# Attention beside an MLP on one core: products with v in groups of four, and all eight PSUM banks given out by a model

## The chip, the cores and the metric

The kernel runs on one core of a Trainium2 chip. The metric is the device time of one execution in microseconds (us), as the median of several executions. The core has engines with a queue of their own each: TensorE (matrix products, PE in the profile; its weight loads are PEld), VectorE (DVE), ScalarE (ACT), GpSimd (POOL), and SyncE (SP), which here only issues DMAs. TensorE writes its products to PSUM, which has eight banks of 128 partitions by 512 float32 numbers. A bank can be written again only when VectorE or ScalarE has read the last product out of it.

## The reference

For 2048 tokens of width 576 the reference computes an attention layer of 32 heads (18 numbers per head) and an MLP of inner width 4608 on the same input, and mixes the two with a gate per token:

```python
def _A_ref(x, wqkv, wo):
    B, S, D = x.shape
    H = 32; Dh = D // H
    qkv = (lambda x, *d: x.transpose(*d))((x @ wqkv).reshape(B, S, 3, H, Dh), 2, 0, 3, 1, 4)
    q, k, v = qkv[0], qkv[1], qkv[2]
    scale = Dh ** -0.5
    scores = jnp.einsum("bhqd,bhkd->bhqk", q, k) * scale
    p = _softmax(scores, axis=-1)
    o = jnp.einsum("bhqk,bhkd->bhqd", p, v)
    return (lambda x, *d: x.transpose(*d))(o, 0, 2, 1, 3).reshape(B, S, D) @ wo

def _B_ref(x, w1, b1, w2, b2):
    y = _layernorm(x, axis=-1)
    h = _gelu(jnp.einsum("bsd,df->bsf", y, w1) + b1)
    return jnp.einsum("bsf,fd->bsd", h, w2) + b2

x = A_x
g = _sigmoid((x * gate_w).sum(-1, keepdims=True))
a = _A_ref(x, A_wqkv, A_wo)
b = _B_ref(x, B_w1, B_b1, B_w2, B_b2)
return g * a + (1 - g) * b
```

## The kernel before

**Stages.** A first stage (to about 245 us) projects q, k and v, prepares the normalized input of the MLP and begins the first MLP products. The main loop carries attention and the MLP together. The rest projects the attention output and mixes (`out_proj`, products on L1353).

**Attention.** The work is cut into 32 units (`NU`): a pair of heads by half of the queries (1024). A unit needs the maximum of every row of scores before its exponentials. So scores are computed twice. A *round* (`s1_round`, products on L234) computes scores for 128 queries by 512 keys for both heads and takes their maxima on VectorE (L236); a unit has 32 rounds. When the last round of a unit has been taken, `s1_finish` turns the maxima into two more rows of the query tile `qa`: `parts` on ScalarE, `rows` on VectorE (L257, L258), and eight small DMAs from the tile `mr` (issued by `dma_r`, L141). They are deferred by counts of *slots*; every call of `run_due` is one slot. With these rows in `qa` the second scores (`s2`, L320) come out with the maximum taken off, and ScalarE's exponential reads them from PSUM and writes the ring buffer (L322). The 512 steps of the main loop are 32 units by 16 blocks of 128 keys; a step has two calls of `s2`, one for each 512 queries. Each call can take a round along (`loop_round`). Rounds run a few calls ahead of the unit that needs them (`LEAD`, 4). When none are left, the kernel calls itself `bare`.

**Products with v** (`pv`, L350) take the exponentials of finished steps and sum them up in one bank per unit. They use the array in another shape: four products of 32 output rows each, side by side, where all score and MLP products use half of the rows each. The ring holds four steps (three from `NARROW` on). In the loop a run of `pv` stands after the first `s2` of a step, in place of an MLP piece. It comes when three steps are finished (`room`, 2 near the end), or when the MLP piece before it ended an MLP unit (`ended`) and at least one step is finished.

**MLP.** It is a generator, `mlp()`. Its units are `h_pair` (two blocks of 128 inner columns, 27 pairs of products on L611, then GELU by ScalarE, VectorE and GpSimd) and `out_pair` (128 tokens by 576, 24 pairs of products on L751, then two additions on VectorE, L721). 36 groups hold two `h_pair` and four `out_pair` each. `fill` draws the next piece after a call of `s2`; where a unit is cut into pieces is set by `ends`. `cut[0]` is 1 at the end of a piece, 2 at the end of a unit, 3 where the next product's input isn't there yet. `spent` and `behind` compare the MLP's progress with its due time.

**Banks.** Six banks are given out by a model (`Earliest`): each has the time at which its reader will be done (`let_go`), by clocks of TensorE, VectorE and ScalarE that the program keeps while it writes the instructions (`pe_t`, `dve_t`, `act_t`). They serve scores, rounds and the sums of `pv`. Two more (`ps_w`) belong to the MLP while rounds are left. The order of instructions on each engine is the one written; semaphores make them wait.

Of the kernel before, what the change touches and what calls it, by code (L numbers as in the profile page):

```python
# [58 lines left out]
NARROW = 431  # L59
# [4 lines left out]
def gated_mix_kernel(ctx: ExitStack, tc: tile.TileContext, x, wqkv, wo, w1, b1, w2, b2, gate_w, out):  # L64
# [97 lines left out]
    def run_due(ns=SLOT):  # L162

        slot[0] += 1
        now[0] += ns
# [74 lines left out]

    def s1_finish(u):
# [7 lines left out]
        def parts():  # L249
# [3 lines left out]
            defer(2 if looped[0] else 8, rows)  # L253

        def rows():
# [11 lines left out]
            for n in range(8):  # L267
                if aside:
                    defer(1 + n, lambda n=n: store(*divmod(n, 4)))
                else:  # L270
                    store(*divmod(n, 4))
        defer(3 if looped[0] else 2, parts)
# [36 lines left out]
    def s2(u, kc, qb, around, ns):  # L309

        flush()
        qa, ka = QA[u % 3], k_tile(UNITS[u][0])
# [26 lines left out]
    def pv(n0, n1):  # L339

        flush()
        for c in range(n0, n1):
# [9 lines left out]
            pe_t[0] += 1040.0  # L352
# [38 lines left out]
    def take_round():  # L391
        u, r = rounds.pop()
        head = s1_round(u, r)
        if r == NR - 1:
            defer(1, lambda: s1_finish(u))
# [10 lines left out]
    lent = [0]  # L406
    extra = [LEAD]
# [12 lines left out]
    def mlp():  # L420
# [129 lines left out]

        def cuts(n, pieces):
# [3 lines left out]
        turns = [0]  # L555

        def pair_of_banks(own):

            if own:
                return [psum(ps_w) for _ in range(2)], ()  # L560
# [6 lines left out]
        def banks(q):  # L567

            if q % 2 and not looped[0]:
                return pair_of_banks(False)  # L570
            return wide_banks()

        def wide_banks():

            if rounds:
                return pair_of_banks(True)
            turns[0] += 1
            return pair_of_banks(turns[0] % 2 == 0)

        def give_back(ids):  # L580
            for b in ids:
                let_go(b, dve_t, 480.0)

        def h_pair(q, last, inner=False):
# [8 lines left out]
            ps, ids = banks(q)  # L593
# [6 lines left out]
            late = spent[0] < behind[0]  # L600
            if room[0] == 3:
                ends = cuts(27, max(1, 5 - piece[0]))
            else:
                ends = cuts(27, (5, 5, 4)[piece[0]] if last else (3, 5, 4)[piece[0]])
                if (last or spent[0] > behind[0] + AHEAD) and piece[0] == 0 and not late:

                    ends = {4, 9, 14, 18, 23}
# [29 lines left out]
            engine(act_t, 690.0)  # L637
            give_back(ids)
# [841 lines left out]
```

## Time and profile before

| | us |
|---|---|
| median of 3 runs | 2214.97 (2214.9 to 2216.17) |
| profiled execution | 2215.03 |
| its span, first to last instruction | 2213.1 |
| ScalarE busy | 1436.3 (65%) |
| VectorE busy | 1644.7 (74%) |
| GpSimd busy | 949.1 (43%) |
| first product with v | at 260.0 |
| last product with v | at 2161.4 |

How to read the profile: the page has the busy time of every engine, groups of instructions by line of the kernel, and what ended the idle time before them. The timeline lists instructions in order of time: start in us, length in us, engine, line, operation, output<-inputs, and how many alike were merged (x8). A number in brackets is idle time of the engine before the instruction, with what released it. Instructions of one shape on both halves of the array run at the same time, so that starts tell more than lengths do. The windows view has, for a stretch, its length and then the busy time (and count) of PE, PEld, DVE, ACT and POOL, the granted TensorE clock (1.00 is full), the DMA share and GB/s.

### The profile page before, as it was taken

Reading aid. Unit: us, or ns where it says so; the run is one execution under the profiler, and the core shown is the slowest. Engines: PE = TensorE matmul, PEld = TensorE weight load, DVE = VectorE, ACT = ScalarE, POOL = GpSimd, SP = SyncE. Lnnn points to the kernel's source line nnn. Section 1 sums busy time; section 2 is a strip of 40 time slices with the busy share of each in tenths; the row PEclk is TensorE's granted clock in tenths of the full one; section 3 lists DMA queues with packets and bytes.
Section 4 is the critical chain, followed back from the end, with each engine's and each line's share of the span. In section 5 each row is a group of like instructions: output and inputs, shape, how many; then the busy total and the mean of one; then the engine's idle time right before and its main releaser. Section 6 shows DMA issues by size and latency. Waiting matters only on the chain. (4 is left out here: it accounts for less than half of the span.)

```text
span 2213.1 us, 51656 instructions
## 1 busy us (share of the span) xinstructions
PE 2196.4 (99%) x20569; PEld 1599.6 (72%) x20569; DVE 1644.7 (74%) x2887; ACT 1436.3 (65%) x2719; POOL 949.1 (43%) x936
## 2 busy tenths in 40 slices
PE   8999999999999999999999999999999999999999
PEld 7878777777767777677677676776677677777668
DVE  5675777777777777777777777777777777787844
ACT  4223677777776666666666666666766667666771
POOL 4002566666663444444445444444534444444420
PEclk9999999999999999999999999999999999999999
DMA  7755654536485423342273424243563333333355
GB/s 241 259 190 188 206 172 140 171 133 179 152 230 184 127 102 122 101 145 92 104 187 141 125 100 124 101 126 120 137 187 113 135 113 106 116 109 117 97 177 182
DMA packets 163414, 323.65 MB, mean 146 GB/s; under 512 B 59838, under 2 KB 86370, under 8 KB 152338
## 3 DMA queue, kind: packets, MB, share of 16 engines
q1 hardware_dynamic: 159462, 313.60, 44.4%
q10 hardware_dynamic: 3712, 6.75, 0.8%
q8 instruction: 162, 2.65, 0.5%
q14 instruction: 78, 0.64, 0.1%
HBM read 229.07 MB, written 95.16 MB: 147 GB/s over the span
## 5 line engine op out<-in xcount | busy, mean ns | idle before, releaser
L236 DVE TENSOR_REDUCE m<-ps 128x1 f32<-128x512 f32 x2048 | 1307.5, 684 | 392.0 <-PE ps L234 354.9
L322 ACT ACTIVATE p<-ps 128x512 f32<-128x512 f32 x1080 | 582.6, 596 | 283.4 <-PE ps L234 188.8
L322 ACT ACTIVATE ring<-ps 128x512 f32<-128x512 f32 x968 | 523.2, 596 | 259.5 <-PE ps L234 186.5
L320 PE MATMUL ps<-qa,ka 56*128 56x512 f32 x2048 | 685.9, 409 | 4.5 <-DMA qa<-mr 2.6
L234 PE MATMUL ps<-ka,qa 54*128 54x512 f32 x2048 | 625.6, 409 | 0.9 <-DVE big L968 0.7
L611 PE MATMUL ps<-big,w 64*128 64x512 f32 x3888 | 516.5, 392 | 0.1
L320 PEld LDWEIGHTS ps<-qa,ka 56*128 56x128 f32 x2048 | 358.4, 185 | 212.0 <-DVE m L236 130.8
L751 PE MATMUL ps<-w,hh 64*128 64x288 f32 x4352 | 491.2, 293 | 0.9 <-ACT z L636 0.8
L187 POOL TENSOR_SCALAR zz<-zz 128x512 f32<-128x512 f32 x272 | 169.2, 622 | 742.7 <-ACT zz L702 714.1
L751 PEld LDWEIGHTS ps<-w,hh 64*128 64x128 f32 x4352 | 418.1, 186 | 22.1 <-ACT z L636 1.2
L611 PEld LDWEIGHTS ps<-big,w 64*128 64x128 f32 x3888 | 380.6, 185 | 72.2 <-ACT vt L1066 0.3
L187 POOL TENSOR_TENSOR zz<-zz,z 128x512 f32<-128x512 f32 x280 | 361.8, 1293 | 35.9 <-ACT zz L705 9.8
L751 PE MATMUL ps<-w,hl 64*128 64x288 f32 x2176 | 340.7, 293 | 0.0
L234 PEld LDWEIGHTS ps<-ka,qa 54*128 54x128 f32 x2048 | 318.2, 186 | 23.1 <-issue 3.6
L350 PE MATMUL ps<-p,vt 128*32 128x512 f32 x2160 | 265.2, 598 | 0.0
L350 PE MATMUL ps<-ring,vt 128*32 128x512 f32 x1936 | 238.9, 598 | 0.0
L751 PEld LDWEIGHTS ps<-w,hl 64*128 64x128 f32 x2176 | 236.9, 186 | 0.0
L187 POOL TENSOR_TENSOR w<-x,w 128x576 fp32r<-128x576 f32 (+1 forms) x34 | 68.2, 2009 | 271.2 <-ACT w L490 206.6
L187 POOL TENSOR_TENSOR hl<-zz,hh 128x512 fp32r<-128x512 f32 x134 | 174.6, 1304 | 14.0 <-ACT hh L664 3.2
L350 PEld LDWEIGHTS ps<-p,vt 128*32 128x32 f32 x2160 | 57.9, 109 | 126.8 <-issue 124.2
L350 PEld LDWEIGHTS ps<-ring,vt 128*32 128x32 f32 x1936 | 52.3, 109 | 112.2 <-issue 111.2
L1037 PE MATMUL ps<-big,wqk 128*128 128x512 f32 x504 | 123.5, 400 | 0.0
(120 smaller groups left out, 1452.0 us busy)
## 6 DMA issues: line engine op xcount, KB each, us to landing
w<-w_scr SPq DMA_DIRECT2D x54, 1152.0 KB
w<-w_scr SPq DMA_DIRECT2D x108, 576.0 KB
w_scr<-w SPq DMA_DIRECT2D x18, 1152.0 KB
w_scr<-w SPq DMA_DIRECT2D x36, 576.0 KB
qa<-qk_scr SPq DMA_DIRECT2D x192, 72.0 KB
ka<-qk_scr SPq DMA_DIRECT2D x90, 144.0 KB
big<-y_scr SPq DMA_DIRECT2D x48, 256.0 KB
x<-in_B_w_dram SPq DMA_DIRECT2D x34, 288.0 KB
```

Source lines behind the costliest of these rows:

```text
L187: fn(*args, **kw)
L234: nc.tensor.matmul(ps, qa[r0:r0 + 54, t * P:(t + 1) * P], ka[r0:r0 + 54, kb * TB:(kb + 1) * TB], start=True, stop=True)
L236: nc.vector.tensor_reduce(M4[u][:, h, t, kb:kb + 1], ps, axis=AX.X, op=ALU.max)
L320: nc.tensor.matmul(ps, ka[r0:r0 + 56, kc * P:(kc + 1) * P], qa[r0:r0 + 56, qb * TB:(qb + 1) * TB], start=True, stop=True)
L322: nc.scalar.activation(ring(n)[:, qb, h], ps, AF.Exp, scale=SCALE)
L350: nc.tensor.matmul(OB[u][0][r:r + 32, :], v[:, k, 19 * h:19 * h + 32], ring(c)[:, qb, h, :], start=(k == 0), stop=(k == NT - 1))
L611: nc.tensor.matmul(ps[h], wt[w_][r, c, :], Y[s_][r, c, :], start=(k == 0), stop=(k == 26))
L751: mm = nc.tensor.matmul(ps[nn][:, :ND], h_[r, tok], w_[p_][r, cs[nn]], start=(k == 0 or bare and k == 3 * G), stop=(k == 6 * G - 1 or bare ...
L1037: nc.tensor.matmul(ps, w_[:, c, ms], big[:, s_, :], start=(k == 0), stop=(k == len(prods) - 1))
```

## The change

The loop no longer puts the run of `pv` where an MLP unit ends. It counts steps alone: `GROUP` 4 below step 432, then 3. The run stands at the end of a step and includes that step. All eight banks are in the model, and the MLP takes its two from it as well. Rounds are no longer tied one to a call: `loop_round` leaves one out when the model sees no four banks free, and `spare_round` puts one in between, so that the lead floats between 6 and 10. `now`, the program's time for deferred work, is TensorE's model clock in the loop. Pieces of the MLP are cut by its progress (`pace`). The parts of `s1_finish` are registered in `FINISH`, and `s2` runs what is left of them before a unit starts.

```diff
-NARROW = 431
+NARROW = 432
+GROUP = 4
+AHEAD_MIN = 6
+AHEAD_MAX = 10
+ENTER = 310.0
+PV_NS = 925.0
@@ run_due @@
-        now[0] += ns
+        now[0] = pe_t[0] if looped[0] else now[0] + ns
@@ s1_finish @@
+    def in_turn(u, n, fn):
+        def once():
+            if once in FINISH[u]:
+                FINISH[u].remove(once)
+                fn()
+        FINISH[u].append(once)
+        defer(n, once)
+
+    def finished(u):
+        while FINISH[u]:
+            FINISH[u][0]()
...
-            defer(2 if looped[0] else 8, rows)
+            in_turn(u, 2 if looped[0] else 4, rows)
...
-        defer(3 if looped[0] else 2, parts)
+        in_turn(u, 3 if looped[0] else 2, parts)
@@ s2 @@
         flush()
+        finished(u)
@@ pv @@
         flush()
+        pe_t[0] += ENTER
...
-            pe_t[0] += 1040.0
+            pe_t[0] += PV_NS
@@ rounds @@
-    def lend_round():
-        if rounds and not lent[0]:
-            next_round()
-            lent[0] = 1
-
-    def loop_round():
-        if lent[0]:
-            lent[0] = 0
-        elif rounds:
-            return take_round()
+    lead = [LEAD]
+    must = [0]
+
+    def fits(n, tol):
+        return sorted(free_at)[n - 1] <= pe_t[0] + tol
+
+    def loop_round():
+        if not rounds:
+            return None
+        if must[0] or lead[0] <= AHEAD_MIN or lead[0] <= AHEAD_MAX and fits(4, 300.0):
+            must[0] = 0
+            return take_round()
+        lead[0] -= 1
+        return None
+
+    def spare_round(n, tol):
+        if rounds and lead[0] < AHEAD_MAX and fits(n, tol):
+            lead[0] += 1
+            next_round()
+            return True
@@ mlp @@
+        def pace():
+            d = spent[0] - behind[0]
+            return 0 if d < 0 else 1 if d < AHEAD else 2
...
-            if own:
-                return [psum(ps_w) for _ in range(2)], ()
+        def wide_banks():
             tiles, ids = [], []
             for _ in range(2):
                 tiles.append(psum(ps_x))
                 ids.append(taken[0])
             return tiles, ids
@@ h_pair @@
-            if room[0] == 3:
-                ends = cuts(27, max(1, 5 - piece[0]))
-            else:
-                ends = cuts(27, (5, 5, 4)[piece[0]] if last else (3, 5, 4)[piece[0]])
...
+            ends = cuts(27, 4 + pace() + (open_pairs[0] if looped[0] else 0))
...
-            engine(act_t, 690.0)
-            give_back(ids)
+            let_go(ids[0], act_t, 690.0)
+            let_go(ids[1], dve_t, 750.0)
@@ out_pair @@
+            ends = {7, 15} if bare else {6, 12} if pace() == 0 else {6, 12, 18}
...
+                        if k == 12 and not bare:
+                            must[0] = 1
+                        elif k == 18 and 18 not in ends and not bare:
+                            spare_round(4, 100.0)
@@ banks @@
-    for i in range(4, 6):
+    for i in range(4, 8):
         bank_x.append(ctx.enter_context(tc.tile_pool(name=f"ps_x{i}", bufs=1, space=PSUM)))
         free_at.append(pe_t[0])
-    ps_w = ctx.enter_context(tc.tile_pool(name="ps_w", bufs=2, space=PSUM))
@@ fill @@
-            ended[0] = atom() == 2
-            piece[0] += 1
-            run_due(max(spent[0] - t, GAP))
+            if atom() == 3:
+                spare_round(4, 100.0)
+            run_due()
@@ main loop @@
+    shift = now[0] - pe_t[0]
+    for clock in (pe_t, act_t, dve_t):
+        clock[0] += shift
+    free_at[:] = [t + shift for t in free_at]
...
-            room[0] = 3 if step < NARROW - 3 else 2
...
             s2(u, kc, 0, loop_round(), 462.0)
-            if step - done[0] >= room[0] or room[0] == 3 and ended[0] and step > done[0]:
-                pv(done[0], step)
-                done[0] = step
-                piece[0] = 0
-                ended[0] = 0
-            else:
-                fill(step)
-            s2(u, kc, 1, loop_round(), 462.0)
-            if not (room[0] == 3 and ended[0]):
+            fill(step)
+            s2(u, kc, 1, loop_round(), 462.0)
+            if step + 1 - done[0] >= (GROUP if step < NARROW else GROUP - 1):
+                spare_round(2, 200.0)
+                pv(done[0], step + 1)
+                done[0] = step + 1
+            else:
                 fill(step)
```

More of the change, by code (lines that the diff above doesn't have):

```diff
@@ L239, in s1_round @@
         return head
+    FINISH = {u: [] for u in range(NU)}
+    def in_turn(u, n, fn):
[8 more added lines that the diff above has]
+            FINISH[u][0]()
     def s1_finish(u):
@@ L565, in pair_of_banks @@
             return tiles, ids
[L567 to L578, printed above, removed]
         def give_back(ids):
             for b in ids:
-                let_go(b, dve_t, 480.0)
+                let_go(b, dve_t, 450.0)
         def h_pair(q, last, inner=False):
@@ L592, in h_pair @@
             del W1[q]
-            ps, ids = banks(q)
+            ps, ids = wide_banks()
             if q == 0:
@@ L599, in h_pair @@
             loaded = 0
-            late = spent[0] < behind[0]
-            if room[0] == 3:
-                ends = cuts(27, max(1, 5 - piece[0]))
-            else:
-                ends = cuts(27, (5, 5, 4)[piece[0]] if last else (3, 5, 4)[piece[0]])
-                if (last or spent[0] > behind[0] + AHEAD) and piece[0] == 0 and not late:
-                    ends = {4, 9, 14, 18, 23}
+            ends = cuts(27, 4 + pace() + (open_pairs[0] if looped[0] else 0))
             for k, (w_, s_, c) in enumerate(slots):
@@ L723, in out_pair @@
             ps, ids = wide_banks()
-            ends = {7, 15} if piece[0] == 0 else cuts(24, max(1, 3 - piece[0]))
-            folded = piece[0] == 0 and not bare
-            if folded:
-                ends = {6, 12}
+            ends = {7, 15} if bare else {6, 12} if pace() == 0 else {6, 12, 18}
             k = 0
@@ L736, in out_pair @@
                 elif turn == 1:
-                    if 3 * G not in ends:
-                        lend_round()
                     turned[0] += 2
@@ L762, in out_pair @@
                         k += 1
-                        if folded and k == 6:
-                            if extra[0]:
-                                extra[0] -= 1
-                            else:
-                                lent[0] = 1
-                        if folded and k == 18:
-                            next_round()
+                        if k == 12 and not bare:
+                            must[0] = 1
+                        elif k == 18 and 18 not in ends and not bare:
+                            spare_round(4, 100.0)
                         if k < 6 * G:
@@ L856, in gated_mix_kernel @@
     cut = [0]
-    piece = [0]
-    room = [2]
     behind = [0.0]
@@ L1328, in out_proj @@
         opened[0] = True
-        banks = 0
         for b in range(NB):
@@ L1342, in out_proj @@
                         if 0 in cut_:
-                            ps[t, n] = psum((ps_x, ps_w)[banks % 2])
-                            own[t, n] = None if banks % 2 else taken[0]
-                            banks += 1
+                            ps[t, n] = psum(ps_x)
+                            own[t, n] = taken[0]
                         for c in cut_:
@@ L1363, in out_proj @@
                                                        op0=ALU.mult, op1=ALU.add)
-                        if own[t, n] is not None:
-                            let_go(own[t, n], dve_t, 480.0)
+                        let_go(own[t, n], dve_t, 480.0)
                         yield 122.5
@@ L1390, in gated_mix_kernel @@
     next(proj)
-    ended = [0]
     def fill(step):
```

8 lines of the change are left out of this document (2 added, 6 removed).

## The prediction

> **What bounds the kernel now.** I read the page's engine shares first, then the waits of TensorE, then the stretches, and last the timeline of TensorE around single instructions. The page, its first engine row:
>
> ```profile
> PE 2196.4 (99%) x20569; PEld 1599.6 (72%) x20569; DVE 1644.7 (74%) x2887; ACT 1436.3 (65%) x2719; POOL 949.1 (43%) x936
> ```
>
> The waits of TensorE (engine, line, what it waited for: total us, times, longest), cut to four rows:
>
> ```profile
> PE ps L320 <- DMA qa<-mr: 2.6, 2, 1.8
> PE ps L320 <- DVE x L721: 1.7, 1, 1.7
> ...
> PE ps L751 <- ACT z L636: 0.8, 1, 0.8
> ...
> PE ps L320 <- ACT p L322: 0.2, 1, 0.2
> ```
>
> The stretches (length, then busy us of PE, PEld, DVE, ACT, POOL, granted clock):
>
> ```profile
> 400.00:1200.00 800.00, 800.00 (x7950) 569.03 (x7944) 618.10 (x1066) 563.63 (x1073) 406.44 (x404) 1.00 0.45 145
> ```
>
> TensorE is the bound: 99% of the span, all 800 of 800 us in the middle of the loop at clock 1.00. There VectorE is busy 77% (618.10 of 800) and ScalarE 70%. So in the loop an edit is worth what it takes out of, or puts into, TensorE's own row. That row can still be shortened without removing one product, because a busy TensorE isn't evenly fast. The timeline of TensorE around a run of products with v (L350; eight records, x8, are one step), first with three steps and then with two:
>
> ```profile
> 305.87 1.06 PE L350 MATMUL ps<-ring,vt 128*32 128x512 f32 x8
> 306.75 1.90 PE L350 MATMUL ps<-p,vt 128*32 128x512 f32 x16
> 308.58 0.50 PE L320 MATMUL ps<-qa,ka 56*128 56x512 f32 x1
> ...
> 327.83 0.40 PE L320 MATMUL ps<-qa,ka 56*128 56x512 f32 x1
> 327.84 0.40 PE L234 MATMUL ps<-ka,qa 54*128 54x512 f32 x1
> 328.16 1.92 PE L350 MATMUL ps<-ring,vt 128*32 128x512 f32 x16
> 330.02 0.50 PE L320 MATMUL ps<-qa,ka 56*128 56x512 f32 x1
> 330.02 0.73 PE L234 MATMUL ps<-ka,qa 54*128 54x512 f32 x2
> 330.36 0.39 PE L320 MATMUL ps<-qa,ka 56*128 56x512 f32 x1
> 330.59 0.43 PE L751 MATMUL ps<-w,hh 64*128 64x288 f32 x4
> ```
>
> Score products come as pairs, one on each half of the rows, and and a pair normally takes 0.23 us until the next products start (330.36 to 330.59). The run of three lasts 308.58 - 305.87 = 2.71 us, the run of two 330.02 - 328.16 = 1.86 us; so **one step of products with v costs 0.85 us, and every run 0.16 us besides** (1.86 - 2 x 0.85). The pair ahead of a run takes 0.33 us (327.83 to 328.16), the first behind it 0.34 us (330.02 to 330.36), some 0.10 us too much each. **A run therefore costs 0.36 us for being a run.** The whole trace has 226 runs on TensorE, 166 of two steps and 60 of three (166 x 2 + 60 x 3 = 512); the first, and the last, in its two pieces:
>
> ```profile
> 260.02 1.92 PE L350 MATMUL ps<-p,vt 128*32 128x512 f32 x16
> ...
> 2159.42 1.06 PE L350 MATMUL ps<-p,vt 128*32 128x512 f32 x8
> 2160.30 1.65 PE L350 MATMUL ps<-ring,vt 128*32 128x512 f32 x8
> ```
>
> **The change, part by part.** *Runs of four.* The new loop counts steps alone: one run per four steps below step 432 (108 runs), then per three up to 510 (26), and one of two behind the loop: 135 runs, 91 fewer. Products, weights and their number stay. 91 x 0.36 = **32.8 us off TensorE's row**. Nothing else was under those 0.36 us, since TensorE is the bound; they go off the span unless TensorE then waits.
>
> *Start of the loop.* The row maxima of unit 0 are finished four slots earlier (4 in place of 8 for `rows`). What that moves, in the timelines of TensorE, VectorE and SP's queue:
>
> ```profile
> 246.68 0.43 PE L751 MATMUL ps<-w,hl 64*128 64x288 f32 x2
> 247.89 0.47 PE L320 MATMUL ps<-qa,ka 56*128 56x512 f32 x1 [0.78 <-DMA qa<-mr]
> 247.89 0.71 PE L234 MATMUL ps<-ka,qa 54*128 54x512 f32 x2
> 250.42 0.79 PE L320 MATMUL ps<-qa,ka 56*128 56x512 f32 x1 [1.82 <-DMA qa<-mr]
> ```
> ```profile
> 242.18 1.29 DVE L236 TENSOR_REDUCE m<-ps 128x1 f32<-128x512 f32 x2 [0.35 <-PE ps L234]
> 243.39 0.18 DVE L257 TENSOR_REDUCE nm<-nm 128x16 f32<-128x32 f32 x1
> 243.67 0.21 DVE L258 STREAM_TRANSPOSE mr<-nm 128x32 f32<-128x32 f32 x1
> ```
> ```profile
> 243.91 5.42 SPq L141 DMA_DIRECT2D qa<-mr  x8
> ```
>
> A turn of the loop ahead has three slots and one round, so four slots put L257, L258 and the eight DMAs ahead of the pair of maxima that starts at 242.18: about 1.3 us of maxima and their 0.35 us of waiting, some 1.8 us with the gap behind. SP's queue takes the eight (5.42 us) that much earlier and passes nothing on which the start waits. The second half's product at 250.42 comes 1.8 us earlier: **-1.8 us**. Behind these waits lies a slow stretch:
>
> ```profile
> 246.40:249.80 3.40, 1.42 (x12) 0.66 (x8) 2.58 (x4) 2.81 (x6) 2.97 (x3) 1.00 0.03 5
> 249.80:260.10 10.30, 9.65 (x59) 7.88 (x63) 5.88 (x11) 7.01 (x13) 4.14 (x4) 0.50 0.71 145
> 2094.40:2097.80 3.40, 1.82 (x22) 1.34 (x20) 2.53 (x7) 3.18 (x7) 0.00 (x0) 1.00 0.01 2
> ```
>
> After 3.4 us with 1.42 us busy the granted clock was 0.50 for 10.3 us, which costs half of it, 5.1 us. A like stretch with 1.82 us busy (third row) was followed by none. With 1.8 us less waiting the first has about 2.3 us busy by the same products, so the drop may go; I leave it in the sum and keep -5.1 us for the range.
>
> *Banks and rounds.* This adds waits that the old trace doesn't show. Before, six banks carried scores, maxima and the output of a unit, and two belonged to the MLP; the run with v stood where an MLP unit ended, so that the two were read out under it. Now a run stands anywhere and eight banks go round: one holds the unit's output, two the open MLP product, two may still wait for the additions (L721) of the last. Three are then left where scores and a round want four. Behind a product that waits stands everything on TensorE, in order. VectorE's and ScalarE's pace, from their timelines:
>
> ```profile
> 1003.59 2.52 DVE L236 TENSOR_REDUCE m<-ps 128x1 f32<-128x512 f32 x4 [0.86 <-PE ps L234]
> 1006.02 0.81 DVE L721 SCALAR_TENSOR_TENSOR x<-ps,x 128x288 f32<-128x288 f32 x2
> ```
> ```profile
> 1002.52 2.12 ACT L322 ACTIVATE ring<-ps 128x512 f32<-128x512 f32 x4 [0.18 <-PE ps L320]
> ```
>
> A maximum takes 0.63 us, a bank's two additions 0.81 us, an exponential 0.53 us. Four steps last about 14.5 us and hold 16 maxima (10.1 us) and some two pairs of additions (1.7 us): 11.8 us of VectorE; its run with v is 4 x 0.85 + 0.36 = 3.8 us, so of the other 10.7 us VectorE must have 1.1 us in hand as the run begins: two full banks. The added spare round ahead of each run is just that. ScalarE's 16 exponentials take 8.5 us. On the mean it fits, but with little room. The price of the new waits is bounded below by nothing (226 old periods show 0.2 us of waiting for an exponential in all; a gain is excluded, since there is no bank wait to remove but the 1.7 us of L721), and above by one maximum for each of the 144 MLP output units, 144 x 0.63 = 91 us. The round is left out or moved where the model sees no bank, with a tolerance of 0.3 us, so I take the value near the lower end: 0.3 us at half of the 36 MLP groups, where a first product must wait for the last GELU and the gap stays empty, 18 x 0.3 = **+5.4 us**.
>
> *The clock of the program's own order* (`now` from TensorE's model) shifts when GELU parts, weights and rows are issued to ScalarE, POOL and SP's queue by some slots. The row parts have a lead of 6 to 10 rounds instead of 4, hence more time before a unit starts; POOL is at 406 of 800 us. I cost it at nothing under TensorE's row; if a chain is late, it is in the +5.4.
>
> *End.* Behind the last run with v only the output projection (L1353) is left, and TensorE is full there:
>
> ```profile
> 2162.00:2188.00 26.00, 26.00 (x196) 25.91 (x196) 12.30 (x24) 3.94 (x7) 0.00 (x0) 1.00 0.69 223
> 2188.00:2213.00 25.00, 21.09 (x158) 20.71 (x156) 10.08 (x20) 1.18 (x3) 0.00 (x0) 0.99 0.34 120
> ```
>
> If the MLP ends some steps later or earlier, its products and those of L1353 change places on the same full row: nothing either way, to within the 4 us that aren't full in the last 25.
>
> **Sum.** -32.8 - 1.8 + 5.4 = -29.2 us on the profiled execution's 2215.03 us (span 2213.1): 2185.8, **2186 us**. The median of the runs, 2214.97, is within 0.1 us of that execution, and the 1.9 us outside the span stay.
>
> **The rivals.**
>
> *A: clean.* No new waits, and the slow stretch goes: 2215.0 - 32.8 - 1.8 - 5.1 = 2175 us. For it: no wait for a bank in 800 us now. Against: VectorE's small reserve.
>
> *B: the banks eat half.* One score in ten waits out the model's 0.3 us tolerance: 1024 x 0.1 x 0.3 = 31 us at most, half of it 15: 2215 - 34.6 + 15 = 2196 us, and up to 2210 where nearly all do. For it: the model takes 580 ns for a maximum, the row says 630.
>
> *C: slower, by one wait.* At the end of an MLP output unit the next score waits until the maxima ahead of L721 on VectorE are through. It decides from 34.6 / 144 = 0.24 us per unit; at one half maximum, 0.32 us, it is 46 us: 2226 us. For it: the run with v no longer covers the read-out. Against: L721's two take 0.81 us and one gap of the MLP lies between.
>
> *D: no change.* A run now holds the step just scored, and its last products need that step's exponentials; were ScalarE 0.25 us late at each of 135 runs, 34 us would go: 2214 us. Against: three steps, 2.5 us, lie ahead of them in the run, four exponentials' time.
>
> *E: the clock.* Many short waits could drop the granted clock, as it did once at 249.8; one drop of 5.1 us per MLP group is 36 x 5.1 = 184 us, some 2364 us. Against it the row at 2094.4: 1.6 us idle in 3.4 and still 1.00. [...]
>
> **How the numbers follow.** Forecast (2180 to 2192) 0.45; A 0.17; B 0.20; C 0.09; D 0.07; E 0.02. Faster by over 0.2% (4.4 us, about what a measurement of this kernel can tell from no change): forecast, A, B, 0.82; same, D, 0.07; slower, C and E, 0.11. The range runs from below A (a run may cost 0.40 us: 91 x 0.04 = 3.6 us more, 2172) to the end of B, 2210; outside are D, C and E, and a little of A and B.
>
> **What would show it.** Right: 135 runs of L350 in the timeline, x32 for four steps, 0.16 us besides 0.85 us a step; TensorE's row still full between 400 and 1200 us; the first score of unit 0 without the 1.82 us wait. Wrong: rows "PE ps L320" or "PE ps L234" waiting for "DVE m L236" or "DVE x L721" in the hundreds (B, C), "PE ps L350" waiting for "ACT ring" (D), a granted clock under 1.00 in the loop (E). A loop as full as now and yet not shorter would mean that the 0.36 us isn't a run's own cost.

## The result, and the profile after

| | before | after |
|---|---|---|
| median, us | 2215.18 (2214.90 to 2216.17, 5 runs) | 2321.30 (2319.14 to 2323.71, 5 runs) |
| span of the profiled execution, us | 2213.1 | 2321.9 |
| first score of the loop starts at | 247.9 | 246.3 |
| from there to the end of the last run with v | 1914.0 | 2002.9 |
| from there to the end of the span | 51.2 | 72.7 |
| runs with v | 226 | 135 |

The changed kernel takes 1.0477 times as long, interval 1.0462 to 1.0493. The prediction, 2186 us and faster with a chance of 0.82, was wrong in its sign. Of the 108.8 us by which the span grew, the loop has 88.9 and the tail 21.5; the start gave 1.6 back.

The changed file has other line numbers: scores are L341 (they were L320), rounds L239 (L234), products with v L372 (L350), the MLP's products L622 and L757 (L611 and L751), GELU L647 (L636), the additions L732 (L721), the out-projection L1351 (L1353). The page after, its first engine row:

```profile
PE 2275.9 (98%) x20569; PEld 1643.6 (71%) x20569; DVE 1635.9 (70%) x2889; ACT 1434.8 (62%) x2719; POOL 944.6 (41%) x936
```

The waits of TensorE after, all above 1 us that lie behind the first stage:

```profile
PE ps L757 <- ACT z L647: 4.7, 23, 0.2
PE ps L1351 <- DVE big L1290: 4.2, 2, 2.8
PE ps L341 <- DMA qa<-mr: 3.1, 3, 2.0
PE ps L341 <- DMA dn<-oe: 2.1, 1, 2.1
PE ps L622 <- DMA big<-y_scr: 2.0, 3, 1.2
PE ps L1351 <- ACT big L1281: 1.9, 1, 1.9
PE ps L1351 <- DVE big L1288: 1.7, 3, 0.6
PE ps L341 <- DVE x L732: 1.3, 1, 1.3
```

And the stretches, in the same columns as before: the middle of the loop, and two short ones inside it.

```profile
400.00:1200.00 800.00, 786.73 (x7422) 551.96 (x7422) 582.15 (x1012) 537.34 (x1023) 387.46 (x383) 0.99 0.43 136
698.50:705.30 6.80, 5.83 (x26) 4.25 (x28) 1.29 (x2) 1.19 (x2) 1.55 (x2) 0.50 0.74 172
1196.90:1203.70 6.80, 6.34 (x45) 6.24 (x47) 3.31 (x6) 2.99 (x5) 2.80 (x3) 0.50 0.63 167
```

The start of the loop, on TensorE and on SP's queue:

```profile
248.93 0.76 PE L341 MATMUL ps<-qa,ka 56*128 56x512 f32 x1 [1.96 <-DMA qa<-mr]
```
```profile
239.77 7.99 SPq L146 DMA_DIRECT2D qa<-mr  x8
```

This is the puzzle of the case. The kernel is 106 us slower, TensorE counts as 98% busy, and these waits add up to some 20 us. Busy time is no measure here: in the same 800 us TensorE got through 7422 instructions in place of 7950. The 528 that are missing take 528 x 800 / 7950 = 53 us at the old rate, and only 800 - 786.73 = 13.3 us of it shows as idle. Some 5 us are the two half-clock stretches (the second lies only in part in these 800 us). The rest is hidden, and the timeline of TensorE shows how, at a change of MLP unit that no run with v covers:

```profile
1440.69 1.09 PE L622 MATMUL ps<-big,w 64*128 64x512 f32 x7
1441.39 0.39 PE L341 MATMUL ps<-qa,ka 56*128 56x512 f32 x1
1441.62 0.39 PE L239 MATMUL ps<-ka,qa 54*128 54x512 f32 x2
1441.86 0.39 PE L341 MATMUL ps<-qa,ka 56*128 56x512 f32 x1
1442.05 0.87 PE L757 MATMUL ps<-w,hh 64*128 64x288 f32 x4
1442.63 0.42 PE L757 MATMUL ps<-w,hl 64*128 64x288 f32 x2
1442.77 0.55 PE L757 MATMUL ps<-w,hh 64*128 64x288 f32 x4
1443.03 0.42 PE L757 MATMUL ps<-w,hl 64*128 64x288 f32 x2
1443.16 0.40 PE L341 MATMUL ps<-qa,ka 56*128 56x512 f32 x1
...
1443.86 1.92 PE L372 MATMUL ps<-p,vt 128*32 128x512 f32 x16
1445.60 1.90 PE L372 MATMUL ps<-ring,vt 128*32 128x512 f32 x16
1447.43 0.50 PE L341 MATMUL ps<-qa,ka 56*128 56x512 f32 x1
1447.43 0.73 PE L239 MATMUL ps<-ka,qa 54*128 54x512 f32 x2
1447.77 0.39 PE L341 MATMUL ps<-qa,ka 56*128 56x512 f32 x1
```

The weight loads, ScalarE and VectorE at that place:

```profile
1442.01 0.18 PEld L757 LDWEIGHTS ps<-w,hh 64*128 64x128 f32 x1 [0.20 <-POOL zz L192]
1442.39 0.29 PEld L757 LDWEIGHTS ps<-w,hh 64*128 64x128 f32 x3 [0.20 <-ACT z L647]
```
```profile
1441.65 0.69 ACT L647 ACTIVATE z<-ps,b1t 128x512 f32<-128x512 f32 x1
1442.24 1.08 ACT L343 ACTIVATE ring<-ps 128x512 f32<-128x512 f32 x2
```
```profile
1440.65 1.29 DVE L241 TENSOR_REDUCE m<-ps 128x1 f32<-128x512 f32 x2 [0.58 <-PE ps L239]
```

Read the starts, not the lengths. Behind the run (1447.43) a score and a round start together, one on each half of the rows. At 1441.39 it is still so: the score starts beside the last product of the old unit (the seventh of the x7), and the round's two products follow together at 1441.62. The next score, at 1441.86, starts alone. The first product of the new unit (L757) starts on the other half only 0.19 us later, and the second at 1442.39, which is 0.53 us behind that score where a pair takes 0.23. One half of the array works while the other waits for a bank, and TensorE counts as busy. The weight load of the second product waits for the GELU of the unit before, which reads its bank until 1441.65 + 0.69 = 1442.34. The first one's starts at 1442.01, just behind a maximum that ends at 1440.65 + 1.29 = 1441.94; that it waits for that maximum's bank is read from this order alone, since the row names an earlier GpSimd instruction. From 1441.39 to 1443.16 pass 1.77 us for two pairs of 0.23 and six of 0.13, 1.25 us; 0.52 us are lost. TensorE's own row shows no idle time there at all, the weight loads twice 0.20 us.

So I worked the loss out from starts, for the whole loop: a stretch goes from one call of `s2` to the next, and its loss is its time less what its products take as pairs (0.233 us for scores, rounds and L622, 0.131 us for L757, 0.85 us for a step with v), less 0.36 us for a run with v in it, of which 0.10 count in the stretch behind the run, whose first pair is that much longer. "Right behind a run" means that a run lies in the stretch before, so that one call of `s2` stands between. From 300 us to 60 us before the last run, in us (in brackets the number of stretches):

| kernel | a unit starts, right behind a run | a unit starts, without | all others |
|---|---|---|---|
| before | -1.5 (202) | 0 (0) | 18.7 |
| after | 0.9 (30) | 64.6 (170) | 81.2 |

**Every one of the 202 MLP units of the old kernel starts right behind a run with v, and loses nothing. Of the new kernel's, 170 start without one and lose 0.38 us each**; 81.2 - 18.7 = 62.5 us more are lost in the other stretches, inside the units; some 10 us of these lie at the two half-clock stretches and the waits for DMAs ahead of them. Together 129.5 us. The loop's difference by itself gives the same: +88.9, to which come the 32.8 us that the 91 runs saved and 8.5 us of out-projection products that left the loop (64 fewer, at 26.00 / 196 = 0.133 us each by the old row of L1353): 130.2 us of new waits.

### The profile page after: what moved, and what is told of

Same layout as the page of the kernel before. It is cut to its first block, busy times and chain, and to the rows that moved or that the text cites. A ratio compares the mean times of both kernels' runs of the same rounds, so it can differ in the third digit from the quotient of the medians.

```text
span 2321.9 us, 51642 instructions
## 1 busy us (share of the span) xinstructions
PE 2275.9 (98%) x20569; PEld 1643.6 (71%) x20569; DVE 1635.9 (70%) x2889; ACT 1434.8 (62%) x2719; POOL 944.6 (41%) x936
## 5 line engine op out<-in xcount | busy, mean ns | idle before, releaser
L341 PE MATMUL ps<-qa,ka 56*128 56x512 f32 x2048 | 783.0, 415 | 8.2 <-DMA qa<-mr 3.1
L239 PE MATMUL ps<-ka,qa 54*128 54x512 f32 x2048 | 578.5, 409 | 5.1 <-DVE big L969 0.7
L622 PE MATMUL ps<-big,w 64*128 64x512 f32 x3888 | 572.2, 397 | 6.2 <-DMA big<-y_scr 2.0
L757 PE MATMUL ps<-w,hh 64*128 64x288 f32 x4352 | 547.5, 300 | 8.0 <-ACT z L647 4.7
L757 PEld LDWEIGHTS ps<-w,hh 64*128 64x128 f32 x4352 | 462.1, 186 | 45.1 <-DVE x L732 14.7
L341 PEld LDWEIGHTS ps<-qa,ka 56*128 56x128 f32 x2048 | 368.9, 185 | 176.3 <-issue 111.0
L622 PEld LDWEIGHTS ps<-big,w 64*128 64x128 f32 x3888 | 410.3, 186 | 91.8 <-ACT z L647 11.2
L757 PE MATMUL ps<-w,hl 64*128 64x288 f32 x2176 | 424.8, 293 | 0.0
L757 PEld LDWEIGHTS ps<-w,hl 64*128 64x128 f32 x2176 | 323.2, 186 | 0.0
L239 PEld LDWEIGHTS ps<-ka,qa 54*128 54x128 f32 x2048 | 286.4, 186 | 46.7 <-DVE m L241 22.6
L372 PE MATMUL ps<-p,vt 128*32 128x512 f32 x2160 | 259.7, 598 | 0.6 <-DVE z L646 0.2
L372 PE MATMUL ps<-ring,vt 128*32 128x512 f32 x1936 | 232.2, 592 | 0.0
L372 PEld LDWEIGHTS ps<-ring,vt 128*32 128x32 f32 x1936 | 63.1, 110 | 144.6 <-issue 142.7
L372 PEld LDWEIGHTS ps<-p,vt 128*32 128x32 f32 x2160 | 56.3, 109 | 121.5 <-issue 114.6
L732 DVE SCALAR_TENSOR_TENSOR x<-ps,x 128x288 f32<-128x288 f32 x270 | 110.1, 449 | 37.0 <-PE ps L757 28.0
```

The lines of the kernel that those rows point to most:

```text
L239: nc.tensor.matmul(ps, qa[r0:r0 + 54, t * P:(t + 1) * P], ka[r0:r0 + 54, kb * TB:(kb + 1) * TB], start=True, stop=True)
L341: nc.tensor.matmul(ps, ka[r0:r0 + 56, kc * P:(kc + 1) * P], qa[r0:r0 + 56, qb * TB:(qb + 1) * TB], start=True, stop=True)
L372: nc.tensor.matmul(OB[u][0][r:r + 32, :], v[:, k, 19 * h:19 * h + 32], ring(c)[:, qb, h, :], start=(k == 0), stop=(k == NT - 1))
L622: nc.tensor.matmul(ps[h], wt[w_][r, c, :], Y[s_][r, c, :], start=(k == 0), stop=(k == 26))
L732: nc.vector.scalar_tensor_tensor(dst, ps[nn][:, :ND], 0.5, b2b[:, cs[nn]] if base else dst, op0=ALU.mult, op1=ALU.add)
L757: mm = nc.tensor.matmul(ps[nn][:, :ND], h_[r, tok], w_[p_][r, cs[nn]], start=(k == 0 or bare and k == 3 * G), stop=(k == 6 * G - 1 or bare ...
```

## The experiments

Four theories stood against each other. **1:** VectorE is late under runs of four, and everything waits for maxima. **2:** the lead lies at its lower end, so that every call takes a round whether there are banks or not, as before, but without the order that suited it. (In the stretches counted, the changed kernel left a round out of 11 calls of 964, the old one of 138 of 963.) **3:** the run with v used to cover the read-out of the old unit's two banks; without it nine banks are wanted of eight (one for the sums, two of the old unit, two of the new, two for scores, two for the round). **4:** the model's times are wrong, so that it gives out banks in a bad order. Each experiment is told as the time of one execution where no interval is given; the old kernel ran beside them at 2215.26 to 2216.66 us. A kernel's losses come from the same reckoning as in the table above.

### Half of a maximum's work

```diff
-            nc.vector.tensor_reduce(M4[u][:, h, t, kb:kb + 1], ps, axis=AX.X, op=ALU.max)
+            nc.vector.tensor_reduce(M4[u][:, h, t, kb:kb + 1], ps[:, :TB // 2], axis=AX.X, op=ALU.max)
```

> The changed kernel, but each maximum reads 256 of a bank's 512 columns, so that a maximum takes VectorE some 0.35 us instead of 0.63 (the row maximum is then taken over half of the keys; order of instructions unchanged). Theory 1 (VectorE is idle under the run of four and has too little time outside it) and theory 2 (a round is tied to nearly every call of s2, also where the MLP piece behind it is only six products) both put the new waits down to VectorE's pace: they go, some 2195 us. Theory 3 (the waits come from banks that the MLP holds, or from ScalarE): stays above 2290 us.

Measured: 2295.80 us, 25.5 less. The middle of its loop:

```profile
400.00:1200.00 800.00, 782.85 (x7519) 548.62 (x7519) 386.93 (x1027) 540.74 (x1033) 385.92 (x381) 1.00 0.44 138
```

VectorE went from 582 to 387 us busy, and TensorE does 7519 instructions, 97 of the 528 that are missing. Starts without a run still lose 57.0 us (170), the others 62.7. Theory 1 has a part, some 25 us, and not the main one: a VectorE with half of its time free doesn't cure the starts.

### Groups of two and of three

```diff
-GROUP = 4
+GROUP = 2
...
-            if step + 1 - done[0] >= (GROUP if step < NARROW else GROUP - 1):
+            if step + 1 - done[0] >= GROUP:
...
+                if step % 4 == 1:
+                    fill(step)
```

(With `GROUP = 3` the first two edits alone.)

> The changed kernel with runs of two steps all along (256 runs; an MLP piece also behind every second run, so that the MLP has as many pieces as with fours). 121 more runs at 0.36 us are +44 us. Theory 1: the waits go with the long run, -129 us, some 2237 us. Theory 2 and theory 3: the waits stay, some 2365 us.

> The changed kernel with runs of three all along (171 runs). 36 more runs are +13 us. Theory 1: VectorE was idle 0.99 us under a run of three against 2.32 under a run of four, so more than half of the waits go, some 2250 us. Theory 2 and theory 3: some 2335 us.

Measured: 2373.56 us with 256 runs, 2346.46 us with 171. Shorter runs, at fixed steps, make it slower, by more than the runs themselves cost: from 135 to 171 runs are 36 x 0.36 = 13 us of the 25.2, to 256 runs 121 x 0.36 = 44 us of the 52.3. In both most units still start without a run in front (161 with three, losing 65.5 us; 146 with two, 60.9). So the long run is not the trouble. More runs don't cure it either, as long as they stand at fixed steps. Both times lie some 10 us above what theories 2 and 3 had foreseen.

### Other piece ends in the MLP

```diff
-            ends = cuts(27, 4 + pace() + (open_pairs[0] if looped[0] else 0))
+            ends = cuts(27, 4 + 2 * pace() + (open_pairs[0] if looped[0] else 0))
...
-            ends = {7, 15} if bare else {6, 12} if pace() == 0 else {6, 12, 18}
+            ends = {7, 15} if bare else {6, 12}
```

> The changed kernel with an output unit of the MLP cut into 6, 6 and 12 products always (a spare round may come in the 12), and the h units into more pieces instead (4 + 2 x pace). Theory 2: the waits at the output units go, some 80 us, 2240 us. Theory 1: VectorE's total outside the runs is the same, the waits move to the h units, 2300 to 2330 us.

Measured: 2295.67 us, 25.6 less: starts without a run 50.5 us (168), the others 70.8. An output unit is now cut in three at most, with a spare round tried at its product 18 each time, and `h_pair` into more pieces when the MLP is ahead; both kinds of loss fall somewhat. Theory 2's 2240 us didn't come, but the spare rounds that it counts on hardly came either: only 17 calls go without a round.

### The run put back where a unit ends, in the new kernel

```diff
-            if atom() == 3:
+            end = atom()
+            ended[0] = end == 2
+            if end == 3:
...
-            fill(step)
+            if ended[0] and step > done[0]:
+                pv(done[0], step)
+                done[0] = step
+                ended[0] = 0
+            else:
+                fill(step)
...
-            if step + 1 - done[0] >= (GROUP if step < NARROW else GROUP - 1):
+            if ended[0] or step + 1 - done[0] >= (GROUP if step < NARROW else GROUP - 1):
```

> The changed kernel, but a run with v also stands wherever an MLP unit has just ended (runs of 1 to 4 steps, 218 in all), as it did before the change. Theory 3 (at a change of MLP unit nine banks are wanted of eight: one for the sums, two of the old unit, two of the new, two scores, two of the round): 83 more runs cost +30 us, the 65 us at unit starts without a run go, and of the other 78 us of new waits a part, 2225 to 2286 us, some 2245. Theory 2 (rounds are tied to calls since the lead lies at its minimum, wherever the units end): the waits stay, some 2350 us.

Measured: 2307.53 us with 218 runs. Its waits, the first two rows:

```profile
PE ps L341 <- DMA qa<-mr: 24.9, 14, 3.3
PE ps L372 <- ACT p L343: 6.7, 1, 6.7
```

The starts are cured: 199 behind a run, together 0.6 us, none without. The time fell only 13.8 us, and theory 3 had 2286 us at most: another wait took the place, 24.9 us for the rows of the next unit, which come too late here with the lead of four rounds. The granted clock was lower too: its mean over the span was 0.989 (after: 0.993). At 0.50 and 1.00 this makes, as an estimate, 0.011 x 2 x 2305.7 = 51 us at half clock in place of 0.007 x 2 x 2321.9 = 33 us, and half of the difference is lost, some 9 us. So the point was open until the lead was mended too:

```diff
-LEAD = 4
+LEAD = 8
-FIN = NSTEP - 6
+FIN = NSTEP - 9
-AHEAD_MIN = 6
-AHEAD_MAX = 10
+AHEAD_MIN = 8
+AHEAD_MAX = 12
```

> run_at_change, but rounds start with a lead of 8 in place of 4 (and keep 8 to 12), so that the rows of a unit are there in time, and the MLP is due three steps earlier (FIN = NSTEP - 9). In run_at_change the waits at unit starts fell from 65 to 0.6 us, but waits for qa<-mr came up (24.9 us) and 8 products of the output projection in place of 96 lay in the loop. Theory 3: without these two the loop is the old one, 2220 to 2245 us. If the new waits have another cause that the runs at unit ends don't touch: above 2270 us.

Measured: 2272.96 us, 48.3 less than after, with 217 runs. The middle of its loop, and its wait for the rows:

```profile
400.00:1200.00 800.00, 796.40 (x7722) 559.84 (x7716) 614.46 (x1052) 555.21 (x1057) 398.94 (x395) 1.00 0.44 139
```
```profile
PE ps L341 <- DMA qa<-mr: 2.5, 1, 2.5
```

Starts behind a run lose nothing (-2.7 us, 200), the others 69.9. The kernel pays 82 x 0.36 = 29.5 us for 82 more runs than after and is yet 48.3 us faster. 300 of the 528 missing instructions are back. This decides for theory 3 as the cause of the loss at unit starts, the largest single part. It doesn't make theory 3 the whole: that had 2220 to 2245 us, and over 2270 was to mean another cause besides. What is left is seen in three places. The loop begins 8.6 us later than after's, as the longer lead has more rounds ahead of it; its 1943.8 us are still 29.8 more than before; and the tail is as long as after's (72.4 us, 32 products of the out-projection in the loop), so that the earlier due end of the MLP didn't shorten it here.

### No round where a unit changes, and rounds elsewhere

```diff
+        if change[0] and not must[0] and lead[0] > AHEAD_MIN:
+            change[0] = 0
+            lead[0] -= 1
+            return None
...
+                elif looped[0] and 6 <= k <= 24 and not spared:
+                    spared = spare_round(4, 100.0)
...
-                        elif k == 18 and 18 not in ends and not bare:
-                            spare_round(4, 100.0)
+                        elif 15 <= k <= 22 and not bare and not spared:
+                            spared = spare_round(4, 100.0)
```

(`change` is set where a unit ended; the piece ends are those of the experiment above. The second kernel, `spares_only`, has all but the first four lines.)

> The changed kernel with runs of four anywhere, but the call of s2 behind the end of an MLP unit takes no round along, and a spare round is tried at every slot in the middle of the units instead. Theory 3: seven banks are wanted at a change, the waits at unit starts go down from 65 us to under 25: 2260 to 2285 us. Theory 2: the gain is that of the spare rounds alone, so the same as spares_only.

> The changed kernel with the spare rounds in the middle of the units as in skip_at_change, and nothing left out at unit ends: the lead can float. Theory 2: the waits go down, below 2285 us. Theory 3: unit starts still want nine banks, as pieces, 2290 to 2320 us.

Measured: 2290.21 and 2305.02 us. Starts without a run: 21.4 us at 161 with the first edit, 0.13 us each; 75.4 us at 168 without it. The 161 are of two kinds. 124 go without the round and lose 0.04 us each; 37 took one all the same, since the lead was at six or the MLP asked for one (`must`), and lose 0.45 us each. So leaving out the round takes two banks out of the nine and nearly the whole loss with them, as theory 3 has it. The price shows elsewhere: the other stretches lose 95.3 us in the first and 55.9 in the second, since the round must be made good there. Beside `pieces`, whose piece ends they share, the spare rounds of `spares_only` took 15 us out of the units (70.8 to 55.9) and put 25 us into the starts (50.5 to 75.4): theory 2 has a part inside the units, and rounds elsewhere are paid for where banks are shortest.

### The end of the MLP

```diff
-FIN = NSTEP - 6
+FIN = NSTEP - 9
```

> The changed kernel with the MLP's due end three steps earlier (FIN = NSTEP - 9). The tail behind the last run with v is 21.5 us longer than before because the MLP ends at step 508 and the output projection then waits for its inputs: if so, 8 to 12 us go, 2309 to 2313 us. If the tail is long for another reason (the state of the queues behind the loop): 2321 us.

Measured: 2308.41 us, 12.9 less. Its last 52 us beside the same of after, cut in five:

```profile
2254.00:2306.00 52.00, 49.23 (x372) 48.81 (x368) 26.52 (x50) 7.21 (x13) 0.00 (x0) 1.00 0.61 205
```
```profile
2249.00:2260.00 11.00, 11.00 (x84) 10.64 (x80) 3.38 (x7) 0.00 (x0) 0.00 (x0) 1.00 0.86 293
2260.00:2268.00 8.00, 4.34 (x17) 3.26 (x17) 6.86 (x12) 3.62 (x6) 0.00 (x0) 0.83 1.00 341
2268.00:2279.00 11.00, 11.00 (x71) 11.00 (x71) 4.83 (x10) 1.79 (x3) 0.00 (x0) 0.81 0.90 322
2279.00:2290.00 11.00, 10.09 (x77) 9.86 (x75) 4.11 (x8) 0.63 (x1) 0.00 (x0) 1.00 0.48 167
2290.00:2322.00 32.00, 25.32 (x176) 24.92 (x176) 14.97 (x28) 4.60 (x8) 0.00 (x0) 0.95 0.37 119
```

After's MLP ended at about step 509, some five steps later than before, so that only 32 products of L1351 found a place in the loop (96 before, 80 here), and the input of the others was late. TensorE waited 7.8 us for it (rows "PE ps L1351" above: 4.2 + 1.9 + 1.7), and the clock fell: 0.17 x 8 + 0.19 x 11 + 0.05 x 32 = 5.1 us by the rows. With the MLP done earlier both are gone, and the tail is 52.3 us (51.2 before, 72.7 after). 8.5 us (moved products) + 7.8 + 5.1 = 21.4 is the tail's 21.5. The gain in time is less than the tail's, as 48 products are back in the loop.

### The model's times

```diff
-MAX_NS = 580.0
-EXP_NS = 490.0
+MAX_NS = 630.0
+EXP_NS = 530.0
...
-ENTER = 310.0
-PV_NS = 925.0
+ENTER = 360.0
+PV_NS = 850.0
```

> The changed kernel with the model's times set to the measured ones: a maximum 630 ns (580), an exponential 530 (490), a step with v 850 (925) and 360 per run (310). Theory 4 (the model hands out the wrong bank because its times are off): more than 40 us go, under 2280 us. Theory 3 (nine banks wanted of eight, whichever is picked): 2305 to 2330 us.

Measured: 2323.12 us, no gain: 68.2 us at 170 starts, 76.3 elsewhere. Theory 4 falls.

### From the other side: runs at fixed steps in the old kernel

```diff
-                ends = cuts(27, max(1, 5 - piece[0]))
+                ends = cuts(27, 6)
...
-            if step - done[0] >= room[0] or room[0] == 3 and ended[0] and step > done[0]:
+            if step - done[0] >= room[0]:
...
-            if not (room[0] == 3 and ended[0]):
-                fill(step)
+            fill(step)
```

> The kernel before, with its eight banks split six and two and its own rounds, but a run with v after every third step wherever that falls, and none for the end of an MLP unit (h units in six pieces, to keep the MLP's progress). 171 runs in place of 226: -20 us. Theory 3: more than half of the unit changes lose the run that covered them, some 120 at 0.38 us or more, +45 to +70 us: 2240 to 2270 us. Theory 2 (the new rounds and their lead are the cause): nothing of that is in this kernel, 2195 us.

Measured: 2394.18 us with 185 runs, 177.5 more than before beside it. Its waits and the middle of its loop:

```profile
PE ps L751 <- DVE x L721: 25.0, 64, 0.6
PE ps L320 <- DVE m L236: 24.1, 33, 1.3
PE ps L751 <- ACT z L636: 11.6, 32, 0.8
PE ps L611 <- DVE x L721: 11.4, 26, 0.6
```
```profile
400.00:1200.00 800.00, 761.50 (x7095) 526.77 (x7095) 565.05 (x975) 515.52 (x982) 356.02 (x349) 1.00 0.39 126
```

Nothing of the new bank model is in it, only the runs' places and pieces cut to fit, and it is slower than the changed kernel. Here the MLP has two banks of its own, so a new unit needs exactly those that the old one still fills: 139 starts without a run lose 123.1 us, 0.89 each, and the waits are long enough to show as idle (rows of L751 and L611 behind L721 and L636). Theory 3 had the mechanism and put the time 124 us too low. Part of that is not at the starts: the other stretches lose some 76 us here, against 18.7 before, with the old rounds and the old split of the banks, so that neither the new rounds nor the bank model is needed for a loss inside the units. How much of it the new cuts make isn't shown. The tail is 18.6 us longer than before.

### What stays after the starts are cured

Both start from `run_at_change2`: one with half of each maximum's work, one with fewer tied rounds and the spare rounds of `out_pair`.

```diff
+        if not must[0] and lead[0] > AHEAD_MIN:
+            lead[0] -= 1
+            return None
```

> run_at_change2 (runs of four at most, and one at every MLP unit's end), with each maximum over 256 of 512 columns. What is left there of new waits, some 50 us inside the units, is VectorE's pace (theory 1): 2230 us or less. Or it is a round with nearly every call of s2 for TensorE's own order of products (theory 2): above 2255 us.

> run_at_change2, output units always cut 6, 6 and 12, a spare round tried at every slot of the 12, and a call of s2 without a round for each spare one. Theory 2: the calls with a round beside output products (336, 40 us of loss) become fewer, 10 to 25 us go: 2248 to 2263 us. Theory 1: VectorE has the same work, 2270 us.

Measured: 2263.76 and 2268.91 us. The stretches without a unit start still lose 60.9 and 61.2 us (69.9 without the edits, 18.7 in the old kernel). So VectorE's pace bears 9 us of this rest and the placing of rounds 9; of the latter 4 reach the time, no more than single executions of the changed kernel differ (2319.1 to 2323.7). Neither theory's forecast was met, 2230 us or less and 2248 to 2263. Were both gains to add up, some 33 us (69.9 - 9.0 - 8.7 - 18.7) would be left; the two edits together weren't tried. As an estimate, some 8 of the 33 lie in `run_at_change2` at two places where TensorE waited for a DMA (1.8 and 2.5 us), with 3.4 us at half clock put down for each; its mean granted clock is 0.995. For the other 25 no run shows a cause.

### The one part that helps: the rows of unit 0

In the old kernel, alone, and one slot in place of the change's four:

```diff
-            defer(2 if looped[0] else 8, rows)
+            defer(2 if looped[0] else 1, rows)
```

> The kernel before, with the rows of unit 0 issued one slot behind their parts instead of eight. The eight DMAs go out some 4 us earlier, the waits of 0.78 and 1.82 us at 247.9 and 250.4 go, -2.6 us; if the granted clock then stays at 1.00 behind 249.8, another -5.1 us. With both 2207 us, with the first alone 2212.5 us.

Measured: 2212.88 us (median of 10) against 2216.66, ratio 0.9982, interval 0.9973 to 0.9992. **It is faster than the kernel before**, by some 4 us. Its two fastest executions (2211.00 and 2211.15) have a mean granted clock of 1.000; the other eight have 0.997 to 0.999, the old kernel's thirteen 0.997 or 0.998. In its profile (the slowest of its ten executions) the second half's score waits a little less and starts 1.12 us earlier (249.30, against 250.42), and the slow stretch has 0.67 in place of 0.50 over the same 10.3 us:

```profile
249.30 0.49 PE L320 MATMUL ps<-qa,ka 56*128 56x512 f32 x1 [1.55 <-DMA qa<-mr]
```
```profile
240.07 8.11 SPq L141 DMA_DIRECT2D qa<-mr  x8
```
```profile
249.80:260.10 10.30, 10.30 (x73) 7.30 (x72) 7.08 (x12) 8.58 (x16) 4.80 (x5) 0.67 0.77 151
```

SP begins 3.84 us earlier (243.91 before) and takes 8.11 us for the eight DMAs instead of 5.42, so that it is done only 1.15 us earlier. Of the 2.69 us more, 1.5 us are a wait until an earlier DMA has landed, `w_scr<-w`, issued at 235.96; the other 1.2 us are in the issues themselves (median 0.61 us before). SP's own wait there:

```profile
SPq L141 <- DMA w_scr<-w: 1.5, 1, 1.5
```

The next experiment took the queue for the cause and gave half of the eight to ScalarE's:

```diff
-                dma_r(nc.scalar if aside else nc.sync, dst, mr[c:c + 16, :])
+                dma_r(nc.scalar if aside or not looped[0] and k % 2 else nc.sync, dst, mr[c:c + 16, :])
```

> rows_early (the kernel before with the rows of unit 0 issued earlier), the eight DMAs of unit 0 now half on SP's queue and half on ScalarE's. In rows_early they took SP's queue 8.11 us and the second score still waited 1.5 us, with the clock down for part of the stretch behind. If the queue is the cause, both go: 2208 us. If not, 2213 us as rows_early.

Measured: 2217.10 (median of 10) against 2216.29, ratio 1.0004, interval 0.9994 to 1.0013: neither forecast came, and the gain is gone again. ScalarE's timeline, its issues in two parts:

```profile
241.49 2.22 ACTq L141 DMA_DIRECT2D qa<-mr  x2
247.58 1.28 ACTq L141 DMA_DIRECT2D qa<-mr  x2
248.91 0.63 ACT L694 ACTIVATE ring<-ring 128x512 f32<-128x512 f32 x1 [6.85 <-DMA qa<-mr]
```

The four issues take 3.5 us of the 7.38 that they hold the engine. Between the second and the third lie 3.87 us; I put them down to the same `w_scr<-w`, issued at 235.87 here, and no row shows that wait by itself. TensorE waits 7.2 us for a GELU that stands behind them. So, read this way, the eight DMAs were held up by the landing of that DMA as well as by their queue, and a kernel without that wait wasn't tried.

## Why the prediction was wrong, step by step

- **What bounds the kernel: right, and read too far.** TensorE is the bound. But "all 800 of 800 us" was taken to mean that nothing waits. A busy array can be one half busy; instructions per stretch say what busy time doesn't.
- **Runs of four: right.** 135 runs, 91 fewer, and the price holds: the run of four above takes 1447.43 - 1443.86 = 3.57 us, 4 x 0.85 + 0.17, the pair ahead of it 0.33, the first behind 0.34. The 32.8 us left TensorE's row. What the step missed is its premise "Nothing else was under those 0.36 us": under each of the old runs at a change of unit lay the read-out of two banks, and **at such a place a run costs about what it hides**, 0.36 against 0.38 us.
- **Start of the loop: the number right, by luck.** -1.6 us for -1.8. But the eight DMAs began 4.14 us earlier (239.77 for 243.91), not 1.8, and took SP's queue 7.99 us instead of 5.42. And the wait of the second half's score, 1.82 us, which was to be gone, is still there with 1.96 at 248.93.
- **Banks and rounds: the step that failed.** The text had the fact ("the run with v stood where an MLP unit ended, so that the two were read out under it") and counted three banks left where four are wanted. Then it priced this at 0.3 us in half of 36 groups, +5.4 us, "near the lower end", because the model leaves rounds out where it sees no bank. It hardly does: 11 calls of 964 went without a round, 138 before, as a round must be taken while the lead is six or less, and the lead grows only by a spare round, for which the model has to see four banks free (two ahead of a run). So nine banks were wanted of eight at nearly every change of unit. A gap of 0.38 us came at 170 unit starts, 64.6 us, and 62.5 us inside the units. (A smaller slip: L721's two additions are one for each of two banks, not two for one.) The mean loads of VectorE and ScalarE ("On the mean it fits") said nothing about eight banks at one place; halving VectorE's work took back 25.5 us.
- **The program's own order: wrong at "I cost it at nothing".** Inputs were late at a few places in the loop (rows "DMA dn<-oe" and "DMA big<-y_scr", 4.1 us), and the two stretches at clock 0.50 that followed cost half of 2 x 6.80, 6.8 us. Nearly all of this is within the 62.5 above.
- **End: wrong.** "nothing either way, to within the 4 us" became +21.5. The moved products were neutral, as said; that their input would be late, and the clock fall on the wait, was not weighed. `fin9` took most of it back.
- **Rivals.** C named the mechanism of the largest term, put the point of decision at 0.24 us per unit and chose 0.32; measured are 0.42 us at 115 output units without a run, and 0.30 us at 55 `h_pair` units, which it didn't count. Its chance of 0.09 was too low, and its time, 2226, lacked the waits inside the units and the end. B's mechanism may be in the rest; no run shows it by itself. D's wait, L372 for an exponential, isn't in the list. E came true in small: four stretches of 3.4 to 6.8 us at half clock behind the loop's start, which cost 6.8 + 5.1 = 11.9 us in all, not one per group. (The row at 2094.4 that stood against it has a counterpart: in `rows_early` the same 3.4 us have 1.88 us busy, and there the clock fell, 0.88 in them and 0.62 in the next 3.4 us.)
- **What would show it: misjudged.** Waiting was to appear as rows in the hundreds of times. It is there, at 170 unit starts, and the waits list has 4.7 us at 23.

What stays open: some 25 us inside the units that neither VectorE's pace, nor the placing of rounds, nor the waits for DMAs and the clock account for, in a kernel whose starts are cured.

## What to carry to other kernels

Before a costly stretch is made rarer, look at what reads, loads or empties beside it at each place where it stands, and count the banks wanted there without it; the gain counts only at places where nothing does. On an array used by halves, compare instructions per stretch and the starts of paired products before a busy share is believed. Where a change has several parts, try the single part alone: of the two tried by themselves in the old kernel, runs at fixed steps lost 177.5 us, and the smallest, unit 0's rows issued earlier, gained some 4.

## What the runs showed of the hardware

- TensorE's busy share hid some 100 of the 129.5 us that the changed kernel's loop lost, because one half of the rows goes on while the other waits (0.53 us at 1441.86, from a score to the second product of the new unit, where a pair takes 0.23): the loop is idle some 21 us more than before, and its half clock costs 6.8 us. With private banks, at 0.89 us per change, more of the waiting became idle time, 800 - 761.50 = 38.5 us in the middle 800 us.
- Half clock came in lengths of 3.4, 6.8 or 10.3 us: 6.80 at 698.5 and at 1196.9, 10.3 at 249.8 before, and 0.67 over those 10.3 us with the rows early, as 6.8 at half clock would give; some 3.4 at 2292.6 after, from 0.88 and 0.62 in the 3.4 us from 2290.00 and from 2293.40. What it takes to fall isn't settled by the busy share. In the changed kernel, in stretches as long as the shortest of these falls, 3.4 us, counted back from the start of a fall, it fell after 2.34 us busy (at 698.53); the other time it stayed after 1.64 (at 2261.84) and fell after the next 1.85 (at 2265.25):

```profile
695.11:698.53 3.42, 2.34 (x14) 1.05 (x10) 1.84 (x3) 2.95 (x6) 2.69 (x3) 1.00 1.06 218
2258.43:2261.84 3.41, 1.64 (x13) 1.41 (x11) 2.07 (x5) 0.58 (x1) 0.00 (x0) 1.00 0.96 283
2261.84:2265.25 3.41, 1.85 (x8) 1.16 (x8) 3.41 (x6) 2.27 (x5) 0.00 (x0) 1.00 0.98 301
```

- A clock that drops by many short waits, rival E's case, didn't come: at 170 bank waits of 0.38 us the loop's clock was 0.99, and the two stretches at 0.50 come with waits for DMAs, 0.61 and 1.21 us at the first and 2.14 us at the second. A longer bank wait goes with a fall in `rows_early`, 1.7 us for the additions of L721 and the 0.88 and 0.62 from 2094.40 on; in the old kernel the clock stayed at 1.00 there, with 1.72 us of the same wait.
- Issuing eight small DMAs took SP 5.42 us at one time and 8.11 us some 4 us earlier, of which 1.5 us were a wait for an earlier DMA to land. Four on ScalarE's queue held ScalarE for 7.38 us, of which 3.87 lie between the second issue and the third.
